# One batch of eight in two halves of d_ff, around its neighbour, with the order of the attention steps written out

## The chip, the cores and the metric

One NeuronCore of one Trainium2 chip runs the whole program. Times are device microseconds; a time of a kernel is the median of several executions, and a profile is one execution more. The engines named are PE (TensorE; PEld is its weight load), DVE (VectorE), ACT (ScalarE), POOL (GpSimd) and SP (the sync engine, whose queue, SPq, issues nearly all DMAs).

## The reference

Attention in two steps with 32 packed queries, then a gated feed-forward layer on all 4608 tokens, everything in float32:

```python
def sm_attn(qq, kk, vv):
    s = scale * np.matmul(qq, kk.transpose(0, 1, 3, 2))
    s = s - np.max(s, axis=-1, keepdims=True)
    a = np.exp(s)
    a = a / (np.sum(a, axis=-1, keepdims=True) + 1e-09)
    return np.matmul(a, vv)
p_packed = sm_attn(p, k, v)                  # 8 batches, 8 heads, 576 tokens, 64 wide
out = sm_attn(q, p_packed, p_packed)
...
g = x @ w_gate                               # x: the attention's rows, 4608 x 512
silu = g * (1.0 / (1.0 + np.exp(-g)))
val = x @ w_val
return (silu * val @ w_out).astype(np.float32)   # d_ff is 1536
```

## The kernel before

**Batches and chunks.** The batches are worked off one after another. d_ff is cut into 12 chunks of 128 columns (`fc`). In each chunk a batch's tokens come as two pieces, A (256 columns) and B (320). `gv_chunk` (L414) makes 12 matmuls for each piece, six for the gate into one PSUM bank and six for the value into a second; the two banks (`ps_gv`, two buffers) are all that there are. The gate bank is freed by ACT's Silu (`sg`, L435), the value bank by DVE's product (`hf`, or `h` where it is kept, L438). The result is split into a high part (`hh`, ACT, L79) and a low part (`hl`, DVE, L85), and `out_mm` (L446) adds it into four accumulators (`acc`) with three matmuls for each 128 tokens.

**The matrix M.** `m_part` (L390) multiplies the packed values with the weights (`w`, L164) and splits the product into `mh` (ACT) and `ml` (DVE). The second attention's weights are `a2h` and `a2l`, so gate and value are products of M and these.

**Weights.** They arrive as 64-bit words and are made into float32 on the core. `f64_convert` (L95) is two passes on ACT (L101, L102) and three on DVE (L103, L104, L105), each over 1024 columns. There are 12 conversions of gate and value weights (`w0` and so on) and 6 of output weights (`wo_f`), which are then split as well, the low part on POOL. Staging tiles (`st`), k and q share four buffers, so a load on SP's queue waits until one is free.

**Batch 0** runs through all 12 chunks of gate and value first and keeps every product (L545 to L567). Each chunk converts a further weight. A second loop (L570 to L583) then makes all output matmuls. **Batches 1 to 7** (L586 on) do the output matmuls of chunk fc-1 between the pieces of chunk fc. `aux_of(b)` (L466) is the next batch's attention as a generator; a step is taken at each `next(aux)`, twice a chunk. Its last step, at L492 to L497, is the second softmax on both halves at once, over 1152 columns. Every other batch ends with 36 matmuls for rows that both of a pair share (L621 to L628, the rest).

**Order.** PE's order is the written one (`manual_schedule`). On the other engines a scheduler places instructions, and `keep_in_program_order` pins one.

Of the kernel before, what the change touches and what calls it, by code (L numbers as in the profile page):

```python
# [26 lines left out]
SC, NSC = 96, 6  # L27
# [14 lines left out]
def tile_pack_attention_swiglu(ctx: ExitStack, tc: tile.TileContext, qT, kT, v, vq, pT, wgv, wout, out):  # L42
# [19 lines left out]

    wide = [True]
    turn = [0]

    def sooner():
        return tc.high_priority(offset=100)

    def ps():
        turn[0] += 1  # L70
        if wide[0] and turn[0] % 2:
            return ps_acc.tile([P, 512], F32, tag="acc", name="acc_aux")
        if wide[0] and turn[0] % 4:
            return ps_gv.tile([P, 512], F32, tag="gv", name="gv_aux")
        return ps_aux.tile([P, 512], F32, tag="aux", name="aux")

    def copy(e, dst, src):
        if e is nc.scalar:
            e.copy(dst, src)  # L79
        else:  # L80
            e.tensor_copy(dst, src)

    def split(dst_h, dst_l, src, hi=nc.scalar, lo=nc.vector):
        copy(hi, dst_h, src)
        lo.tensor_tensor(dst_l, src, dst_h.bitcast(F32), op=ALU.subtract)  # L85
# [4 lines left out]
    def f64_load(src):  # L90
        st = io_tile([P, 1024, 2], I32, "st")
        nc.sync.dma_start(st.rearrange("p n two -> p (n two)"), src)
        return st

    def f64_convert(dst, st, shape):  # L95

        lo, hi = (st[:, :, i].rearrange("p (a n) -> p a n", a=shape) for i in range(2))
        d = dst.bitcast(I32)  # L100
        nc.scalar.activation(dst, hi.bitcast(F32), AF.Abs)  # L101
        nc.scalar.activation(lo.bitcast(F32), lo.bitcast(U32), AF.Identity, bias=minus_two, scale=LOW_WORD)  # L102
        nc.vector.tensor_scalar(dst, dst, F64_HI_LEAST, F64_HI_MOST, op0=ALU.max, op1=ALU.min)  # L103
        nc.vector.scalar_tensor_tensor(d, d, 3, lo, op0=ALU.logical_shift_left, op1=ALU.bitwise_or)  # L104
        nc.vector.scalar_tensor_tensor(d, hi, 0x3FFFFFFF, d, op0=ALU.bitwise_or, op1=ALU.bitwise_and)  # L105
# [6 lines left out]
    def convert_w(fc):  # L112
        f64_convert(w_t[fc // 2][:, :, fc % 2, :], sts.pop(fc), NHP)

    def load_wout(fc):
        sto[fc] = io_tile([P, 1024, 2], I32, "st")
        nc.sync.dma_start(
# [3 lines left out]
    def convert_wout(fc):  # L121
        f = wos[fc] = pool.tile([P, 2, DM], F32, tag="wf", bufs=1, name="wo_f")
        f64_convert(f, sto.pop(fc), 2)

    def slot(dtype, name):
        return pool.tile([P, DM], dtype, tag="slot", bufs=2 * NFC + 2, name=name)
# [11 lines left out]
    def load_k(b):  # L138
        p_t = pool.tile([P, NHP, NP], F32, tag="p", bufs=2, name="p_t")
        (nc.sync if b else nc.scalar).dma_start(p_t, pT[b])  # L140
        k_t = io_tile([P, 2, NHP, HS], F32, "k_t")
        for hf in range(2):
            nc.sync.dma_start(k_t[:, hf], kT[b, :, hf])
        kps[b] = (k_t, p_t)

    def load_v(b):
        if b < NEARLY:
            vs[b] = pool.tile([SC, NSC, H * D], F32, tag="v", bufs=1, name="v_t")
            nc.sync.dma_start(vs[b], v[b])
        else:  # L150
            vs[b] = pool.tile([P, NPAR, NHP, NKQ, D], F32, tag="v", bufs=1, name="v_t")
            nc.sync.dma_start(vs[b], vq[b - NEARLY])

    def load_q(b):
        qs[b] = io_tile([P, 2, NHP, HS], F32, "q_t")
        for c in range(2):
            nc.sync.dma_start(qs[b][:, c], qT[b, :, c])
# [8 lines left out]
    def s1_scores(b, direct):  # L166
# [21 lines left out]
        if direct:  # L188
# [6 lines left out]
            nc.vector.tensor_tensor(rs[:, 0], rs[:, 1], rs[:, 2], op=ALU.add)  # L195
# [8 lines left out]
    def s1_post(b):  # L204
        t1, rs, _ = st1.pop(b)
        nc.vector.tensor_scalar(rs[:, 1], rs[:, 0], 1e-9, None, op0=ALU.add)
        nc.vector.reciprocal(rs[:, 2], rs[:, 1])
        a1 = pool.tile([SC, NPAR * NSC, P], F32, tag="a1", bufs=1, name="a1")
        for i in range(0, NPAR * NSC, 4):
            p_t = ps()  # L210
            for x in range(4):
                par, c = divmod(i + x, NSC)
                nc.tensor.transpose(p_t[:SC, x * P : (x + 1) * P], t1[:, par, c * SC : (c + 1) * SC], ident)
            copy(
                nc.vector if wide[0] and i == 4 else nc.scalar,
                a1[:, i : i + 4], p_t[:SC].rearrange("p (c x) -> p c x", x=P),
# [4 lines left out]
        for par in range(NPAR):  # L221
            for c in range(NSC):
                for hp in range(NHP):
# [3 lines left out]
                        a1[:, par * NSC + c, 32 * hp : 32 * hp + 32],  # L227
                        v_t[:, c, h * D : (h + 1) * D],
                        start=(c == 0),
                        stop=(c == NSC - 1),  # L230
                    )
        pp = pool.tile([P, NPAR, D], F32, tag="pp", bufs=1, name="pp")
# [9 lines left out]
        ppts[b] = pool.tile([P, P], F32, tag="ppt", bufs=2, name="ppt")  # L242
        nc.scalar.copy(ppts[b], p_t[:, :P])
        yield

    sq = {}

    def q_scores(b):
# [7 lines left out]
        for g in range(2):  # L256
# [12 lines left out]
            for par in range(NPAR):  # L269
                x, m = pss[par][:, : 2 * SQ].rearrange("p (h n) -> p h n", h=2), z[:, 0, par, hs]  # L270
                nc.vector.tensor_reduce(m, x, axis=AX.X, op=ALU.max)
                nc.vector.tensor_tensor(
                    e[:, par, hs, :SQ], x, m.unsqueeze(2).broadcast_to([P, 2, SQ]), op=ALU.subtract
                )
            yield

    def q_weights(b):
# [3 lines left out]
        ev = e.rearrange("p r h n -> p (r h) n")  # L281
        nc.scalar.activation(ev[:, :, :SQ], ev[:, :, :SQ], AF.Exp, scale=SCALE)
        zv = z.rearrange("p s r h -> p s (r h)")
        nc.vector.tensor_reduce(zv[:, 1], ev[:, :, :SQ], axis=AX.X, op=ALU.add)
        x = pool.tile([P, NJ, 2, H], F32, tag="x1", bufs=1, name="x1")
        zd = dram.tile([P, 2, H], F32, tag="zd", bufs=2, name="zd")
        nc.sync.dma_start(zd, zv)
        for i in range(NJ):
            nc.sync.dma_start(x[NP * i : NP * i + NP], zd.rearrange("(j n) s h -> n j s h", j=NJ))
        for _ in range(3):  # L290
# [15 lines left out]
        nc.vector.tensor_tensor(f, t, y[:, 0, NJ], op=ALU.mult)
        nc.vector.tensor_tensor(
            ev[:, :, :SQ], ev[:, :, :SQ], f.unsqueeze(2).broadcast_to([P, H, SQ]), op=ALU.mult
        )
        a1 = pool.tile([P, NPAR, NHP, NKQ, NP], F32, tag="a1", bufs=1, name="a1")  # L310
        for par in range(NPAR):
            nc.vector.transpose(
                a1[:, par].rearrange("p h k n -> p (h k n)"), e[:, par].rearrange("p h n -> p (h n)")
            )
        sq[b] = a1
        for _ in range(2):
            yield
# [20 lines left out]
    def s2_scores(b):  # L338
        s2, _ = st2[b]
        q_t, ppt = qs.pop(b), ppts[b]  # L340
        for c in range(2):
# [5 lines left out]
            for par in range(NPAR):  # L347
                nc.vector.transpose(s2[:, c, par], pss[par][:, :HS])
# [12 lines left out]
    def s2_max(b, cs):  # L361
        x, (m, _, _), shape = s2_view(b, cs)
        nc.vector.tensor_reduce(m, x, axis=AX.X, op=ALU.max)  # L363
        nc.vector.tensor_tensor(x, x, m.unsqueeze(2).broadcast_to(shape), op=ALU.subtract)  # L364

    def s2_exp(b, cs):
        x = st2[b][0][:, cs].rearrange("p c r n -> p (c r n)")
        nc.scalar.activation(x, x, AF.Exp, scale=SCALE)
# [4 lines left out]
    def s2_norm(b, cs):  # L373
        x, (m, s, r), shape = s2_view(b, cs)
        nc.vector.tensor_reduce(s, x, axis=AX.X, op=ALU.add)  # L375
        nc.vector.tensor_scalar(m, s, 1e-9, None, op0=ALU.add)
        nc.vector.reciprocal(r, m)
        nc.vector.tensor_tensor(x, x, r.unsqueeze(2).broadcast_to(shape), op=ALU.mult)  # L378

    def s2_back(b, c):  # L380
# [3 lines left out]
        nc.vector.transpose(t.rearrange("p r n -> p (r n)"), s2[:, c].rearrange("p r n -> p (r n)"))  # L384
        at = (slice(None), slice(None), slice(c * HS, (c + 1) * HS))
        split(ah[at], al[at], t)

    ms = {}

    def m_part(b, k, fcs):  # L390
# [11 lines left out]
        for par in range(NPAR):  # L402
            at = (slice(None), par, fcs)
            split(mh[at], ml[at], pss[par][:, :n].rearrange("p (f n) -> p f n", n=2 * P))
# [3 lines left out]
    def h_split(src, hi, lo):  # L408
        hh = pool.tile([P, 256], F32R, tag="hh", bufs=3, name="hh")
        hl = pool.tile([P, 256], F32R, tag="hl", bufs=3, name="hl")  # L410
        split(hh, hl, src, hi, lo)
        return hh, hl

    def gv_chunk(b, fc, is_b, fill, kept=None):  # L414
# [20 lines left out]
        nc.scalar.activation(sg[:, :n], pgs[0][:, :n], AF.Silu)  # L435
        hf = pool.tile([P, 256], F32, tag="hf", bufs=2, name="hf") if kept is None else kept
# [7 lines left out]
    def out_mm(acc, hh, hl, c, fc):  # L444
        for i, (h_, w_) in enumerate(((hl, wo_h), (hh, wo_l), (hh, wo_h))):
# [4 lines left out]
                start=(fc == 0 and i == 0),  # L450
                stop=(fc == NFC - 1 and i == 2),
            )

    def emit_out(acc, row, eng):
        ot = pool.tile([P, DM], F32, tag="ot", bufs=2, name="ot")
        copy(nc.scalar if eng else nc.vector, ot, acc)
        nc.sync.dma_start(out[row : row + P, :], ot)
# [3 lines left out]
    def run_all(*gens):  # L461
        for g in gens:
            for _ in g:
                pass

    def aux_of(b):  # L466

        d = b + 1
        if d == B:
            return  # L470
        if d < NEARLY:
            yield from s1_scores(d, False)
            if d + 1 < B:
                load_k(d + 1)
# [3 lines left out]
        else:  # L478
            yield from q_scores(d)
            yield from q_weights(d)  # L480
            if d + 1 < B:
# [4 lines left out]
        if d + 1 < B:  # L486
            load_v(d + 1)
        s2_tiles(d)
        yield from s2_scores(d)
        if d + 1 < B:  # L490
            load_q(d + 1)
        s2_max(d, both)  # L492
        s2_exp(d, both)
        s2_norm(d, both)
        s2_a2(d)
        for c in range(2):
            s2_back(d, c)  # L497

    with tc.manual_schedule(engines={mybir.EngineType.PE}):

        load_k(0)
        load_w(0)
        load_v(0)
        load_q(0)
        load_w(1)
        s1 = s1_post(0)
        run_all(s1_scores(0, True))
        for _ in range(3):
            next(s1)
        convert_w(0)  # L510
        run_all(s1)
        load_w(2)
        s2_tiles(0)
        s2_a2(0)
        run_all(s2_scores(0))
        for c in range(2):
# [149 lines left out]
```

## Time and profile before

| | us |
|---|---|
| median of 3 runs (797.18 to 799.49) | 799.23 |
| the profiled execution, its own time | 797.01 |
| its span | 795.2 |
| from the start to batch 0's first gate matmul | 30.09 |
| batch 0, chunks, then outputs | 30.09 to 109.78, to 150.90 |
| batch 1 | 150.90 to 239.63 |
| the rest of batches 0 and 1 | 239.63 to 247.79 |
| batch 2 | 247.79 to 335.91 |
| batch 7, no attention beside it | 705.23 to 783.20 |

The span is what the profile covers; the execution's own time is 1.8 us longer. A stretch is read by its length against PE's busy time in it. PE's order is fixed, so an idle PE names the work that was late.

### The profile page before, as it was taken

The numbers are of one execution on the slowest core, as the hardware profiler recorded it, in microseconds if no ns is written. First come the engines' busy times: TensorE is split into PE (matmuls) and PEld (weight loads), VectorE is DVE, ScalarE is ACT, GpSimd is POOL, SyncE is SP. The second block draws the span as 40 slices with busy tenths as digits, with TensorE's granted clock in tenths as the row PEclk, the third lists the DMA queues.
The fourth block names the chain that finished last, engine by engine and source line by source line (L and its number), as shares of the span: only waits on it lengthen the run. The fifth ranks groups of instructions, "written<-read, shape, count | busy, mean of one in ns | idle before, by whom it ended". The sixth has DMA issues, their size and how long they took to land.

```text
span 795.2 us, 14294 instructions
## 1 busy us (share of the span) xinstructions
PE 743.4 (93%) x5866; PEld 599.5 (75%) x5866; DVE 454.1 (57%) x968; ACT 349.8 (44%) x665; POOL 19.5 (2%) x25
## 2 busy tenths in 40 slices
PE   5579789999999999999999999999999999999998
PEld 3357567787788877878788777878778877888886
DVE  3998777455745656355745557455554556443434
ACT  3688664453532625354432445335442444343331
POOL 0001122000000000000000000000000000000000
PEclk9999998999999999999999999999999999999999
DMA  9957742221101230021101211010101000010001
GB/s 316 305 202 266 259 161 74 100 66 67 61 1 67 66 106 22 27 92 68 60 1 67 67 67 61 1 55 3 68 1 53 16 2 1 2 54 2 1 1 66
DMA packets 19776, 59.09 MB, mean 74 GB/s; under 512 B 5952, under 2 KB 6976, under 8 KB 17216
## 3 DMA queue, kind: packets, MB, share of 16 engines
q1 hardware_dynamic: 19568, 58.12, 20.9%
q8 instruction: 46, 0.75, 0.4%
q14 instruction: 18, 0.15, 0.1%
q10 hardware_dynamic: 144, 0.07, 0.0%
HBM read 48.69 MB, written 9.49 MB: 73 GB/s over the span
## 4 chain that ended last, share of the span: by engine, by line
PE 72%; DVE 15%; ACT 8%; DMA 2%; issue 2%; POOL 0%; SPq 0%; DVEq 0%; ACTq 0%
PE gv L428 31%; PE acc L446 27%; PE aux L164 6%; PE aux L446 4%; DVE ml L85 2%; PE aux L325 2%; DMA v_t<-in_v 2%; DVE r L375 1%; DVE s L378 1%; DVE r L363 1%; ACT L435 1%; DVE s L364 1%; DVE w L104 1%; PE aux L262 1%; DVE hf L438 1%
## 5 line engine op out<-in xcount | busy, mean ns | idle before, releaser
L428 PE MATMUL gv<-a2h,ml 128*128 128x256 f32 (+1 forms) x768 | 175.8, 311 | 28.4 <-DVE t L441 9.2
L428 PEld LDWEIGHTS gv<-a2h,ml 128*128 128x128 f32 x768 | 128.8, 191 | 65.6 <-issue 23.0
L428 PE MATMUL gv<-a2l,mh 128*128 128x256 f32 (+1 forms) x768 | 166.7, 299 | 0.9 <-DVE a2l L85 0.9
L428 PE MATMUL gv<-a2h,mh 128*128 128x256 f32 (+1 forms) x768 | 166.1, 298 | 0.0
L435 ACT ACTIVATE sg<-gv 128x256 f32<-128x256 f32 x192 | 78.8, 411 | 191.2 <-PE gv L428 140.0
L446 PE MATMUL acc<-wo_h,hl 128*128 128x512 f32 x384 | 157.0, 409 | 4.1 <-DVE hl L85 4.1
L438 DVE TENSOR_TENSOR hf<-gv,sg 128x256 f32<-128x256 f32 x168 | 71.1, 423 | 155.8 <-PE gv L428 153.1
L446 PE MATMUL acc<-wo_l,hh 128*128 128x512 f32 x384 | 151.8, 395 | 0.0
L446 PE MATMUL acc<-wo_h,hh 128*128 128x512 f32 x384 | 151.1, 394 | 0.0
L79 ACT CAST hh<-hf 128x256 fp32r<-128x256 f32 x168 | 68.1, 405 | 143.4 <-DVE hf L438 143.4
L428 PEld LDWEIGHTS gv<-a2l,mh 128*128 128x128 f32 x768 | 125.4, 192 | 1.5 <-DVE a2l L85 1.5
L428 PEld LDWEIGHTS gv<-a2h,mh 128*128 128x128 f32 x768 | 125.6, 192 | 0.0
L446 PEld LDWEIGHTS acc<-wo_h,hl 128*128 128x128 f32 x384 | 72.8, 189 | 51.1 <-issue 35.7
L85 DVE TENSOR_TENSOR hl<-hf,hh 128x256 fp32r<-128x256 f32 x168 | 70.4, 419 | 52.8 <-ACT hh L79 52.8
L446 PEld LDWEIGHTS acc<-wo_h,hh 128*128 128x128 f32 x384 | 72.7, 189 | 16.7
L446 PEld LDWEIGHTS acc<-wo_l,hh 128*128 128x128 f32 x384 | 72.9, 190 | 9.5
L85 DVE TENSOR_TENSOR ml<-aux,mh 128x512 fp32r<-128x512 f32 (+1 forms) x106 | 63.0, 630 | 13.1 <-ACT mh L79 12.9
L164 PE MATMUL aux<-w,ppt 64*32 64x512 f32 (+1 forms) x848 | 56.1, 564 | 4.2 <-ACT t L184 4.0
L79 ACT CAST mh<-aux 128x512 fp32r<-128x512 f32 (+1 forms) x106 | 52.2, 546 | 8.0 <-PE aux L164 2.9
L435 ACT ACT_TABLE_LOAD x21 | 26.9, 1283 | 0.7
L102 ACT ACTIVATE st<-st,minus_two 128x1024 f32<-128x1024 uint32 x18 | 22.4, 1246 | 0.6 <-DMA st<-in_wout 0.6
L164 PEld LDWEIGHTS aux<-w,ppt 64*32 64x32 f32 x848 | 10.4, 106 | 13.5 <-ACT t L184 5.0
(127 smaller groups left out, 591.2 us busy)
## 6 DMA issues: line engine op xcount, KB each, us to landing
st<-in_wgv SPq DMA_DIRECT2D x12, 1024.0 KB, 6.0
k_t<-in_kT SPq DMA_DIRECT2D x16, 576.0 KB, 4.9
q_t<-in_qT SPq DMA_DIRECT2D x16, 576.0 KB, 4.7
out<-ot SPq DMA_DIRECT2D x36, 256.0 KB, 2.1
v_t<-in_vq SPq DMA_DIRECT2D x6, 1280.0 KB, 5.7
st<-in_wout SPq DMA_DIRECT2D x6, 1024.0 KB, 6.1
v_t<-in_v SPq DMA_DIRECT2D x2, 1152.0 KB, 12.6
p_t<-in_pT SPq DMA_DIRECT2D x7, 64.0 KB, 3.0
```

The source lines that it names most:

```text
L79: e.copy(dst, src)
L85: lo.tensor_tensor(dst_l, src, dst_h.bitcast(F32), op=ALU.subtract)
L102: nc.scalar.activation(lo.bitcast(F32), lo.bitcast(U32), AF.Identity, bias=minus_two, scale=LOW_WORD)
L104: nc.vector.scalar_tensor_tensor(d, d, 3, lo, op0=ALU.logical_shift_left, op1=ALU.bitwise_or)
L164: nc.tensor.matmul(outs[par][32 * hp : 32 * hp + 32], lhs(r, hp), rhs(r, hp), start=True, stop=True)
L262: nc.tensor.matmul(pss[par][NP * j : NP * j + NP, i * SQ : (i + 1) * SQ], p_t[r, 2 * g + i, :], k_t[r, j // 2, 2 * g + i, j % 2 * SQ : j % ...
L325: nc.tensor.matmul(p_p[D * par : D * par + D, NP * hp : NP * hp + NP], v_t[:, par, hp, k, :], a1[:, par, hp, k, :], start=(k == 0), stop=( ...
L363: nc.vector.tensor_reduce(m, x, axis=AX.X, op=ALU.max)
L428: nc.tensor.matmul(pg[:, :n], m_[:, g, f, s * P : (s + 1) * P], a_[:, g, off : off + n], start=(i == 0), stop=(i == 5),)
L435: nc.scalar.activation(sg[:, :n], pgs[0][:, :n], AF.Silu)
L438: nc.vector.tensor_tensor(hf, pgs[1][:, o : o + 256], sg[:, o : o + 256], op=ALU.mult)
L446: nc.tensor.matmul(acc[:, :], h_[:, c : c + P], w_[fc], start=(fc == 0 and i == 0), stop=(fc == NFC - 1 and i == 2),)
```

## The change

1. **Batch 0 in two halves.** Chunks 0 to 5 of batch 0 run first, with the output matmuls two chunks behind and attention 1 in between; the four accumulators are copied out and written to DRAM (`part`). Batch 1 follows with all 12 chunks. Then batch 0's chunks 6 to 11; `part` is read back and added when its rows are written.
2. **Conversions.** Six of the twelve gate and value weights and half of the output weights are converted ahead of or in the first half; the others one step at a time in batch 1 (`convert_some`), two or three steps at a tick.
3. **Prologue.** DVE's and ACT's order is written out. v comes ahead of the first weight, on 128 partitions in place of 96. 29 matmuls on the identity (`warm_up`) stand where PE waits.
4. **Later attentions.** Their DVE, ACT and DMA instructions are pinned. Both softmaxes are cut in halves, one step a tick, and each exponential follows a Silu (`late`). That makes five exponentials a batch in place of three.

```diff
+    def pin(ins):
+        return tc.keep_in_program_order(ins) if steady[0] else ins
...
+            late.append(lambda hs=hs: pin(nc.scalar.activation(e[:, :, hs, :SQ], e[:, :, hs, :SQ], AF.Exp, scale=SCALE)))
...
         nc.scalar.activation(sg[:, :n], pgs[0][:, :n], AF.Silu)
+        if late:
+            late.pop(0)()
...
-        s2_max(d, both)
-        s2_exp(d, both)
-        s2_norm(d, both)
...
+        for c in halves:
+            s2_max(d, c)
+            late.append(lambda c=c: s2_exp(d, c))
+            yield
+        low = lambda: None
+        for c in halves:
+            low()
+            s2_sums(d, c)
+            yield
+            s2_scale(d, c)
+            low = s2_back(d, c.start)
+            yield
...
+        lo, hi = range(NFC // 2), range(NFC // 2, NFC)
...
             gv_chunk(0, fc, False, fill, kept[fc][:, :256])
+            if fc > 1:
+                outs_kept(fc - 2, 0, h, fill)
+                h = split_kept(fc - 2, 1)
             gv_chunk(0, fc, True, fill, kept[fc][:, 256:])
...
+        part = dram.tile([P, 4, DM], F32, tag="part", bufs=1, name="part")
+        for i in range(4):
+            emit_out(accs[i], part[:, i], i % 2)
...
+        def tick_one(fc, n):
+            convert_some(3 if n == 8 else 2)
...
+            if fc > 6:
+                next(aux)
...
+        whole(1, range(NFC), accs, tick_one, lambda: m_part(0, len(lo) // 2, both))
...
+        back = io_tile([P, 4, DM], F32, "part")
+        load(back, part)
...
+        whole(0, hi, accs, lambda fc, n: next(aux, None), lambda: m_part(2, 0, both))
```

In the rows below a name's number is its buffer; line numbers of the changed kernel are its own. DVE ahead of batch 0's second chunk, before:

```order
L85 TENSOR_TENSOR a2l_224<-t2_283,a2h_223 128x2x288
L85 TENSOR_TENSOR ml_253<-aux_339,mh_252 128x256
L85 TENSOR_TENSOR ml_253<-aux_340,mh_252 128x256
L438 TENSOR_TENSOR h0_306<-gv_332,sg_353 128x256
L103 TENSOR_SCALAR w1_82<-w1_82 128x4x256
L104 SCALAR_TENSOR_TENSOR w1_82<-w1_82,st_287 128x4x256
```

And now:

```order
L423 TENSOR_TENSOR a2l_96<-t2_322,a2h_95 128x2x288
L118 SCALAR_TENSOR_TENSOR w0_81<-st_111,w0_81 128x4x256
L115 TENSOR_SCALAR w1_82<-w1_82 128x4x256
L116 SCALAR_TENSOR_TENSOR w1_82<-w1_82,st_155 128x4x256
L118 SCALAR_TENSOR_TENSOR w1_82<-st_155,w1_82 128x4x256
L115 TENSOR_SCALAR w1_82<-w1_82 128x4x256
L430 TENSOR_TENSOR ml_254<-aux_378,mh_253 128x256
L116 SCALAR_TENSOR_TENSOR w1_82<-w1_82,st_290 128x4x256
L430 TENSOR_TENSOR ml_254<-aux_379,mh_253 128x256
```

The low parts of M for the second chunk came right behind `a2l`; now six passes of three conversions stand in between or ahead of the second of them. PE at the end of batch 0's chunks, before:

```order
L428 MATMUL gv<-a2h,ml 128x320 x2
L428 MATMUL gv<-a2l,mh 128x320 x2
L428 MATMUL gv<-a2h,mh 128x320 x2
L428 MATMUL gv<-a2h,ml 128x320 x2
L428 MATMUL gv<-a2l,mh 128x320 x2
L428 MATMUL gv<-a2h,mh 128x320 x2
L164 MATMUL aux<-q_t,ppt 32x288 x8
L446 MATMUL acc<-wo_h,hl 128x512
L446 MATMUL acc<-wo_l,hh 128x512
```

And in the third chunk of the first half now:

```order
L183 MATMUL aux<-w_82,ppt 32x256 x8
L474 MATMUL gv<-a2h,ml 128x256 x2
L474 MATMUL gv<-a2l,mh 128x256 x2
L474 MATMUL gv<-a2h,mh 128x256 x2
L494 MATMUL acc<-wo_h,hl 128x512
L494 MATMUL acc<-wo_l,hh 128x512
L494 MATMUL acc<-wo_h,hh 128x512
L494 MATMUL acc<-wo_h,hl 128x512
L494 MATMUL acc<-wo_l,hh 128x512
L494 MATMUL acc<-wo_h,hh 128x512
L183 MATMUL aux<-k_t,p_t 32x288 x8
```

Output matmuls, all behind the last chunk before, now stand between the pieces. ACT in batch 2, at the second softmax of attention 3, before:

```order
L435 ACTIVATE sg_3162<-gv_3132 128x256
L368 ACT_TABLE_LOAD
L368 ACTIVATE s2_3029<-s2_3029 128x1152
L79 CAST mh_3146<-aux_3148 128x512
L79 CAST mh_3146<-aux_3149 128x512
L79 CAST hh_3166<-hf_3164 128x256
L435 ACT_TABLE_LOAD
L435 ACTIVATE sg_3190<-gv_3176 128x320
```

And now:

```order
L481 ACTIVATE sg_3252<-gv_3238 128x320
L401 ACT_TABLE_LOAD
L401 ACTIVATE s2_3148<-s2_3148 128x576
L91 CAST hh_3258<-hf_3255 128x256
L481 ACT_TABLE_LOAD
L481 ACTIVATE sg_3300<-gv_3270 128x256
L401 ACT_TABLE_LOAD
L401 ACTIVATE s2_3148<-s2_3148 128x576
L447 CAST mh_3284<-aux_3286 128x512
L447 CAST mh_3284<-aux_3287 128x512
L91 CAST hh_3305<-hf_3303 128x256
L481 ACT_TABLE_LOAD
```

One exponential of 1152 columns became two of 576 behind two Silus that follow each other, each with a table load on either side.

## Rows read from the trace of the kernel before

**Rows 1.** Busy time by stretches, whole core: start and end, length, then for each engine busy us (and instructions), the granted clock, the DMA share and GB/s. The stretches are the prologue, batch 0's first chunk, its other eleven, its outputs, batch 1, the rest, batch 2, batch 7.

```profile
0.00:30.09 30.09, 11.49 (x189) 6.63 (x189) 16.98 (x34) 15.64 (x27) 0.74 (x7) 1.00 0.96 332
30.09:38.07 7.98, 7.04 (x41) 5.41 (x41) 7.95 (x14) 3.60 (x7) 0.00 (x0) 1.00 0.75 220
38.07:109.78 71.71, 58.60 (x600) 44.55 (x598) 59.01 (x107) 53.60 (x92) 9.04 (x7) 0.95 0.65 230
109.78:150.90 41.12, 37.04 (x168) 28.49 (x161) 28.55 (x43) 19.43 (x36) 8.67 (x6) 0.92 0.28 102
150.90:239.63 88.73, 86.76 (x706) 70.28 (x705) 49.93 (x112) 38.98 (x75) 0.20 (x1) 1.00 0.16 57
239.63:247.79 8.16, 8.16 (x39) 6.76 (x38) 3.48 (x9) 0.59 (x1) 0.00 (x0) 1.00 0.30 110
247.79:335.91 88.12, 86.31 (x707) 70.12 (x706) 48.68 (x108) 37.88 (x73) 0.20 (x1) 1.00 0.15 49
705.23:783.20 77.97, 77.88 (x513) 66.68 (x513) 31.08 (x76) 25.93 (x60) 0.00 (x0) 1.00 0.04 15
```

**Rows 2.** Who waited for whom, PE alone, whole span: the waiting instruction, what ended the wait, us in total, times, longest us.

```profile
PE gv L428 <- DVE t L441: 9.2, 6, 1.5
...
PE gv L428 <- ACT sg L435: 4.7, 6, 1.8
PE gv L428 <- DVE h L438: 4.2, 5, 1.4
PE acc L446 <- DVE hl L85: 4.1, 1, 4.1
```

**Rows 3.** DVE's groups by line and shape, whole span: busy us, mean ns of one, and idle time before.

```profile
L104 DVE SCALAR_TENSOR_TENSOR w<-w,st 128x1024 int32<-128x1024 int32 x12 | 14.7, 1221 | 0.9 <-ACT st L102 0.7
L105 DVE SCALAR_TENSOR_TENSOR w<-st,w 128x1024 int32<-128x1024 int32 x12 | 14.6, 1214 | 0.1
...
L438 DVE TENSOR_TENSOR h<-gv,sg 128x256 f32<-128x256 f32 x24 | 10.0, 417 | 5.1 <-PE gv L428 4.2 <-ACT sg L435 1.0
...
L384 DVE STREAM_TRANSPOSE t<-s 128x576 f32<-128x576 f32 x16 | 12.3, 768 | 0.0
...
L103 DVE TENSOR_SCALAR w<-w 128x1024 f32<-128x1024 f32 x12 | 9.1, 768 | 4.1 <-ACT w L101 4.1
L85 DVE TENSOR_TENSOR ml<-aux,mh 128x256 fp32r<-128x256 f32 x22 | 8.5, 419 | 0.4 <-ACT mh L79 0.2
...
L375 DVE TENSOR_REDUCE r<-s 128x18 f32<-128x576 f32 x2 | 1.5, 746 | 0.0
```

**Rows 4.** DVE in order of time in the prologue: start, us, instruction.

```profile
22.45 0.42 DVE L85 TENSOR_TENSOR ml<-gv_aux,mh 128x256 fp32r<-128x256 f32 x1
22.79 0.41 DVE L85 TENSOR_TENSOR ml<-acc_aux,mh 128x256 fp32r<-128x256 f32 x1
...
34.19 1.18 DVE L105 SCALAR_TENSOR_TENSOR w<-st,w 128x1024 int32<-128x1024 int32 x1
...
37.67 1.23 DVE L104 SCALAR_TENSOR_TENSOR w<-w,st 128x1024 int32<-128x1024 int32 x1
```

**Rows 5.** PE in order of time in batch 0: the second chunk's first piece, and a wait with what follows it (in brackets the idle time before and what ended it).

```profile
38.07 0.40 PE L428 MATMUL gv<-a2h,ml 128*128 128x256 f32 x2
...
59.78 0.95 PE L164 MATMUL aux<-w,ppt 64*32 64x256 f32 x16 [2.10 <-ACT t L184]
...
61.95 0.73 PE L428 MATMUL gv<-a2h,ml 128*128 128x320 f32 x2
```

**Rows 6.** ACT's waits, whole span: the copy of an accumulator waiting for its output buffer.

```profile
ACT ot L79 <- DMA out<-ot: 11.5, 8, 2.3
```

**Rows 7.** PE in order of time: a whole part of M, the scores and the packing of a later attention.

```profile
710.17 1.09 PE L164 MATMUL aux<-w,ppt 64*32 64x512 f32 x16
159.01 1.25 PE L262 MATMUL aux<-k_t,p_t 64*32 64x144 f32 x32
280.42 2.52 PE L325 MATMUL aux<-a,v_t 128*64 128x32 f32 x80
```

**Rows 8.** DVE and PE in order of time in batch 2, at the second softmax.

```profile
304.77 1.34 DVE L378 TENSOR_TENSOR s<-s,r 128x1152 f32<-128x1152 f32 x1
306.03 0.42 DVE L438 TENSOR_TENSOR hf<-gv,sg 128x256 f32<-128x256 f32 x1
307.39 0.47 PE L428 MATMUL gv<-a2h,ml 128*128 128x256 f32 x2 [1.54 <-DVE t L441]
```

**Rows 9.** ACT in order of time in batch 2, at the first softmax's exponential.

```profile
261.54 0.38 ACT L435 ACTIVATE sg<-gv 128x256 f32<-128x256 f32 x1 [2.06 <-DVE z L271]
261.94 1.28 ACT L282 ACT_TABLE_LOAD   x1
263.23 1.17 ACT L282 ACTIVATE e<-e 128x1152 f32<-128x1152 f32 x1
264.30 0.39 ACT L79 CAST hh<-hf 128x256 fp32r<-128x256 f32 x1
264.71 1.28 ACT L435 ACT_TABLE_LOAD   x1
266.00 0.44 ACT L435 ACTIVATE sg<-gv 128x320 f32<-128x320 f32 x1
```

**Rows 10.** SP's queue in order of time in batch 2: maxima and sums go to DRAM (zd) and come back (x).

```profile
265.81 0.33 SPq L287 DMA_DIRECT2D zd<-z  x1
267.75 1.75 SPq L289 DMA_DIRECT2D x<-zd  x4
```

More of the change, by code (lines that the diff above doesn't have):

```diff
@@ L26 @@
 NFC = DF // P
-SC, NSC = 96, 6
+NSC = -(-S // P)
 NJ, SQ = 4, S // 4
@@ new lines, in begin, with rest @@
+    def begin(b):
+        odd = b % 2
+        if b // 2 not in t4:
+            t4[b // 2] = pool.tile([P, NFC, P], F32, tag="t4", bufs=1, name="t4")
+        row0 = (b // 2) * 2 * S
+        rows = [row0 + P * t for t in ((7, 8, 5, 6) if odd else (0, 1, 2, 3))]
+        return rows, [ps_acc.tile([P, 512], F32, tag="acc", name="acc") for _ in range(4)]
+    def rest(b):
+        p4 = ps()
+        t4_t = t4.pop(b // 2)
+        for fc in range(0, NFC, 2):
+            h = h_split(t4_t[:, fc : fc + 2].rearrange("p f t -> p (f t)"), nc.vector, nc.vector)
+            for i in range(2):
+                out_mm(p4, *h, i * P, fc + i)
+        row = (b // 2) * 2 * S + 4 * P
+        emit_out(p4, out[row : row + P], 0)
@@ new lines, in tile_pack_attention_swiglu, with convert_some @@
+        work = None
+        asked = 1
+        def convert_some(n):
+            nonlocal work, asked
+            for _ in range(n):
+                while work is None or next(work, 0) == 0:
+                    if not todo:
+                        return
+                    while asked < min(len(todo), 3):
+                        todo[asked][0](todo[asked][2])
+                        asked += 1
+                    work = todo.pop(0)
+                    asked -= 1
+                    work = work[1](work[2])
@@ new lines, in tile_pack_attention_swiglu, with then @@
+        _, accs = begin(0)
+        back = io_tile([P, 4, DM], F32, "part")
+        load(back, part)
+        load_k(3)
+        whole(0, hi, accs, lambda fc, n: next(aux, None), lambda: m_part(2, 0, both))
+        run_all(aux)
+        load_q(3)
+        for i, r in enumerate(rows):
+            emit_out(accs[i], out[r : r + P], 0, back[:, i])
+        rest(1)
+        for b in range(2, B):
+            rows, accs = begin(b)
+            if b + 1 < B:
+                aux = attention(b + 1)
+            def then():
+                if b + 1 < B:
+                    m_part(b + 1, 0, both)
+            whole(b, range(NFC), accs, lambda fc, n: next(aux, None), then)
```

485 lines of the change are left out of this document (275 added, 210 removed).

## The prediction

> **What bounds the kernel now.** I read the windows by stage first, PE's waits second, then the order of time inside the stages where PE waits, and last the groups of DVE and ACT, which give prices. In the windows [rows 1], compare PE's busy time with the length of each stretch. Batch 7, with nothing beside it, takes 77.97 us, 77.88 of them busy at a granted clock of 1.00: PE is the bound there and nothing on another engine can help. Batch 2 is 8.43 us busier (attention 3 and a part of M) and loses 1.8 us. The loss sits at the start: 30.09 us until the first gate matmul, then 79.7 us for chunks that hold about half of batch 0's matmuls. In 38.07 to 109.78 PE is idle for 71.71 - 58.60 = 13.1 us, and the clock of .95 says that some of its busy time was at the lower level too. DVE is busy 59.01 us there, ACT 53.60: neither is full, yet PE waits on both. In batch 0's outputs PE is idle 4.1 us more, in one wait for the low part of a kept product [rows 2]. So batch 0 costs 30.09 to 150.90 = 120.8 us, where a bare batch costs 78.
>
> PE's other waits are small: 9.2 us in six for `t`, the second half of the softmax's product [rows 2]. Batch 2 shows what lies behind one: a pass of 1.34 us over 1152 columns stands ahead of the product that frees the value bank, and PE idles 1.54 us [rows 8].
>
> **The change part by part.**
>
> *Start to batch 0's second chunk.* It begins at 38.07 [rows 5]. v arrives earlier, so the first exponential does, and the first chunk's first piece may begin some 4 us sooner. But PE's second chunk needs the low part of M, and ahead of that DVE still has its list: by 38 us it had finished three conversions and begun a fourth [rows 4]; now three whole ones and two passes of a fourth stand ahead. The list is the same, so I take 38 as unchanged; bounds 35 to 41 (the gain of the early piece at most; or one conversion, 0.77 + 1.22 + 1.21 = 3.20 us [rows 3], more). The 29 warm-up matmuls stand where PE is free (11.49 us busy of 30.09 [rows 1]) and cost nothing; without that cover they would cost some 3 us, at half of the .20 that one of 256 columns takes [rows 5].
>
> *First half, from 38 us to batch 1.* DVE's list here: five conversions of 3.20 and one last pass, 17.2 us; 31 products and low parts of .42, 13.0; six products of the shared rows at half that, 1.3; two softmax halves, each four passes like the 746 ns reduce, two like the 768 ns transpose and .4 of small ones, 9.8; eight maxima and transposes of 288 columns, estimated at .46 each, 3.7; small ones .9. Together 45.9 us over 82 instructions, at the durations of [rows 3]. Neighbours overlap: two low parts of .42 start .34 apart [rows 4]; .08 on each of 82 leaves 39.3. In the stretch before, with the same mix of work, DVE was busy 59.01 of 71.71 us [rows 1], a share of .823. At that share the list takes 39.3/.823 = 47.8 us with the overlap taken off, 45.9/.823 = 55.8 without, so batch 1 would begin at 86 or 94. PE has about half a batch, 39 us, and some attention, so it isn't the bound. ACT's list is about as long as DVE's. At the end four accumulators are copied out through two buffers; ACT has waited up to 2.3 us for such a buffer [rows 6]. Batch 1 uses the same banks, so I add one for that to the middle, 90: batch 1's first gate matmul at **91**, range 84 to 97 (109.78 + 41.12 after it was the old end of the whole batch).
>
> *Batch 1.* A bare batch, 77.97 [rows 1]; a whole part of M for batch 0's second half, 1.09; two groups of scores of attention 2, 2 x 1.25 [rows 7]: 81.6 us of PE. Six conversions and half of the output weights are beside it. DVE has 49.93 us in batch 1 before [rows 1]; six conversions add 19 and part of an attention leaves, so 65 to 74 of some 85, where the first loop ran at .82. In that loop a value bank was needed back after 12 matmuls of the next piece; here output matmuls lie between, so each eviction has about 78/24 = 3.2 us. Idle time for this: from 0 to the 13.1 us that the first loop lost over eleven converting chunks. I take 4, since the spacing is roughly double. Batch 1: 85.6, to 176.6.
>
> *Batch 0's second half.* Half of 77.97, 39.0; a part of M for batch 2, 1.09; packing 2.52; the product with q at 1.25 [rows 7]; and what is left of an attention's 8.43 us, 1.07. Sum 44.9, to 221.5. The read of `part` (1 MB) is asked for well ahead and DMA is busy for a sixth of such a stage [rows 1]: nothing. The adds replace copies on DVE. Then the rest, 8.16 as before: 229.7 in place of 247.79, so **-18.1**.
>
> *Batches 2 to 6.* The 1.34 us pass becomes two, and `t` no longer stands behind it: the 1.8 us that a batch loses falls to about .6, five times -1.2 = **-6**; bounds -8.5 (all of it) and +4 (the new stalls below). The exchange through DRAM keeps its length: zd is issued at 265.81 and the last of x at about 269.5 [rows 10], and the reduction that waits for x is now pinned about one chunk, 6.5 us, behind; if x is late, the products queued behind it on DVE wait about a microsecond, which the second value bank covers. ACT gets two more exponentials a batch, with two more loads before and two after them: 4 x 1.28 = 5.1 us [rows 9] on an engine busy 37.88 of 88.12 [rows 1].
>
> The row bears on that last price: the Silu after the exponential's load pair starts 4.46 us after the one before, and PE doesn't wait for it; the exponential starts as its load ends, 261.94 + 1.28 = 263.22 [rows 9].
>
> The Trainium skill, page "ScalarE: Activation LUTs", section "What ACT_TABLE_LOAD costs", gives each switch about 2.66 us, a load of 1283 ns and then a drain of 1380, and its section on table sets wants calls of one set batched, which speaks against cutting exponentials in halves between Silus. The load agrees with the row; the drain isn't seen there. By the page ACT would get 10.6 us a batch rather than 5.1, and the Silus around a pair would be late.
>
> *The last batch* has no attention beside it: nothing changes.
>
> Sum: -18.1 - 6 = -24.1. The profiled execution took 797.01 us, so 772.9, rounded to **773**; it lies 2.2 us below the median of the runs, 799.23, which I leave in the range.
>
> **The rivals.**
>
> *All engines keep pace.* DVE's list then runs without gaps (43 us from 38: batch 1 at 81), batch 1 has no stalls and batches 2 to 6 lose nothing: 773 - 10 - 4 - 2.5 = 756. For it: conversions no longer stand in PE's way in the written order. Against: in the old loop DVE never passed .82.
>
> *The split exponentials surface on PE.* Two half exponentials follow each other, one for each Silu. A piece then costs ACT .38 + 1.28 + .59 + .39 + 1.28 = 3.9 us [rows 9], two 7.8, against a chunk of 6.5 on PE; with two casts of M, .8, ACT is 2.1 behind. Before, the spare bank hid such a delay. If it doesn't, two pairs a batch lose 4.2 in place of 1.8: 5 x 2.4 = +12 in place of -6, so 791. By the section on table sets in the Trainium skill, page "ScalarE: Activation LUTs", this is what would happen, with drains on top.
>
> *It doesn't do what it says.* The conversions in the first half, with a whole attention and maxima between them, keep PE waiting as in the old loop, and batch 1 starts at 109 as the outputs did: +18, 791.
>
> *Slower: the conversions pinned into batch 1 hold its evictions.* In the old loop a 2.10 us wait is followed by matmuls of 320 columns at .73 where the .40 of 256 columns gives .50 [rows 5]: the lower clock. If each of nine converting chunks has one such wait and some 3.4 us at half rate after it (1.7 lost), batch 1 loses 9 x 3.8 = 34 in place of 4: +30, 803. It decides from (4 + 26)/9 = 3.3 us lost in each converting chunk. Against it: .42 us products wait for at most one conversion pass, 1.22 us, since two or three passes stand at a tick with products between.
>
> **How the numbers follow.** Forecast 773, with its own range of 764 to 782: .53. All keep pace, 756: .17. Split exponentials, 791: .12. Not what it says, 791: .10. Slower, 803: .06. Within 0.3% (2.4 us, about what a measurement of this kernel can tell from no change): .02. The range takes in the forecast's own and, two us beyond 756 and 791, most of the fast case and of the two middle rivals: 754 to 793. Faster by over 0.3%: .53 + .17 + .12 + .10 = .92; slower .06.
>
> **What would show it.** Right: second chunk near 38, batch 1's first gate matmul near 91, end of the rest near 230, batches 2 to 6 some 87 us each, and PE's wait for `t` gone from its list. If batch 1 starts past 100, the first half is as bound by the conversions as the old loop was; a clock under .95 there says that PE's gaps cost twice. Many waits of PE on `h` or `sg` in batch 1 mean that conversions stand ahead of evictions. ACT's Silu named as releaser in batches 2 to 6, at pairs of table loads, means that the split cost more than the pass of 1152. It would be wrong altogether if PE were busy for less of the first half than of the old loop, 58.60 of 71.71 us.

## The result and the profile after

The changed kernel takes 803.76 us (median of 4 runs, 803.33 to 804.35) against 798.25 for the kernel before beside it (797.18 to 799.49): ratio 1.008, 95% interval 1.0062 to 1.0098. It is slower by 0.8%, and the interval lies clear of 1. The forecast of 773 and its range, up to 793, missed. The profiled execution took 803.33 us, its span 801.5.

Windows by stage of the changed kernel, columns as in [rows 1]: prologue and first pieces, the second chunk on, batch 1, batch 0's second half, the rest, batch 2, batch 7.

```profile
26.01:37.88 11.87, 6.95 (x44) 4.84 (x42) 11.45 (x18) 8.30 (x11) 0.00 (x0) 0.71 0.47 170
37.88:104.74 66.86, 52.74 (x427) 38.15 (x427) 48.51 (x88) 41.96 (x72) 9.87 (x7) 0.87 0.30 105
104.74:200.60 95.86, 87.33 (x593) 70.97 (x593) 64.03 (x123) 57.05 (x95) 7.63 (x6) 0.93 0.38 133
200.60:247.25 46.65, 44.42 (x377) 35.80 (x376) 27.58 (x64) 21.21 (x40) 0.20 (x1) 1.00 0.35 134
247.25:255.53 8.28, 8.28 (x36) 6.83 (x37) 4.19 (x12) 0.00 (x0) 0.00 (x0) 1.00 0.23 87
255.53:343.46 87.93, 86.76 (x705) 70.42 (x704) 49.49 (x116) 43.09 (x79) 0.20 (x1) 1.00 0.14 48
711.24:789.38 78.14, 78.05 (x513) 66.83 (x512) 31.12 (x76) 25.92 (x60) 0.00 (x0) 1.00 0.04 14
```

Set against the forecast's own stages:

| stage | forecast, us | measured, us | off |
|---|---|---|---|
| second chunk begins | 38 | 37.88 | 0 |
| batch 1's first gate matmul | 91 | 104.74 | +13.7 |
| batch 1 | 85.6 | 95.86 | +10.3 |
| batch 0's second half and the rest | 44.9 + 8.16 | 46.65 + 8.28 | +1.9 |
| start of batch 2 to start of batch 7 | 457.4 - 6 | 455.71 | +4.3 |

The last batch adds 0.2 (78.14 for 77.97). Together 30.4, and 772.9 + 30.4 = 803.3. Batch 2 begins at 255.53 in place of 247.79, 7.7 us late; batches 2 to 6 give back 1.7.

PE's waits in the changed kernel, whole span, as in [rows 2]:

```profile
PE gv L474 <- ACT sg L481: 10.0, 14, 3.8
PE acc L494 <- DVE hl L95: 4.6, 4, 2.8
PE gv L474 <- DVE h L486: 4.0, 2, 2.9
...
PE aux L183 <- ACT t L203: 3.1, 1, 3.1
PE aux L183 <- DVE w L118: 1.8, 1, 1.8
```

The wait for `t` of [rows 2], 9.2 us, is gone as forecast (the `t` of L203 is another tile). In its place Silu (`sg`) is late 14 times for 10.0 us, where it had been 4.7 in six: three times in batch 1, once in batch 0's second half, and twice in each of batches 2 to 6. One of these is 3.8 us long, in batch 1. ACT there, in order of time, and then windows before, in and after the stretch that follows:

```profile
166.34 0.41 ACT L91 CAST hh<-hf 128x256 fp32r<-128x256 f32 x1 [1.60 <-DVE hf L486]
166.65 1.13 ACT L111 ACTIVATE w<-st 128x1024 f32<-128x1024 f32 x1
167.68 1.21 ACT L113 ACTIVATE st<-st,minus_two 128x1024 f32<-128x1024 uint32 x1
168.90 1.28 ACT L306 ACT_TABLE_LOAD   x1
170.20 0.68 ACT L306 ACTIVATE e<-e 128x576 f32<-128x576 f32 x1
170.90 1.28 ACT L481 ACT_TABLE_LOAD   x1
172.19 0.44 ACT L481 ACTIVATE sg<-gv 128x320 f32<-128x320 f32 x1
```

```profile
164.00:171.00 7.00, 4.50 (x23) 3.41 (x21) 3.70 (x8) 5.34 (x8) 0.00 (x0) 0.99 0.39 152
171.00:181.00 10.00, 6.56 (x32) 4.32 (x33) 6.90 (x12) 6.08 (x9) 0.00 (x0) 0.50 0.01 1
181.00:200.00 19.00, 19.00 (x119) 16.22 (x119) 12.94 (x32) 9.37 (x18) 2.54 (x2) 1.00 0.02 3
```

From 166.34 to the Silu at 172.19 ACT has 5.9 us of work in a row: a cast, two passes of a conversion, and an exponential with a table load on either side, none of them waiting for another engine once the cast has begun. PE runs dry, and then works ten microseconds at a granted clock of .50, the 1.2 GHz level.

The first half, cut in three:

```profile
38.00:61.00 23.00, 16.17 (x112) 11.06 (x113) 20.89 (x30) 15.50 (x23) 5.19 (x3) 0.71 0.67 232
61.00:86.00 25.00, 23.08 (x253) 17.40 (x253) 15.18 (x34) 16.50 (x34) 4.47 (x4) 1.00 0.12 44
86.00:105.00 19.00, 13.63 (x67) 9.76 (x66) 12.58 (x26) 10.09 (x17) 0.20 (x1) 0.91 0.08 28
```

DVE is full first (20.89 of 23 us), then PE (23.08 of 25), then nobody: the second softmax of attention 1 goes from engine to engine. Here a transpose on DVE is cast on ACT, the low part of it waits for that cast, and behind it stands the low part that PE waits for:

```profile
92.20 0.77 DVE L420 STREAM_TRANSPOSE t<-s 128x576 f32<-128x576 f32 x1
93.01 0.67 ACT L422 CAST a2h<-t 128x576 fp32r<-128x576 f32 x1 [1.66 <-DVE t L420]
93.71 0.76 DVE L423 TENSOR_TENSOR a2l<-t,a2h 128x576 fp32r<-128x576 f32 x1 [0.74 <-ACT a2h L422]
94.39 0.75 DVE L95 TENSOR_TENSOR hl<-h,hh 128x256 fp32r<-128x256 f32 x2
94.86 0.50 PE L494 MATMUL acc<-wo_h,hl 128*128 128x512 f32 x1 [2.77 <-DVE hl L95]
```

No average over the half shows that.

### The profile page after: what moved, and what is told of

Its sections match the earlier page's. It is cut to its first block, busy times and chain, and to the rows that moved or that the text cites. A ratio compares the mean times of both kernels' runs of the same rounds, so it can differ in the third digit from the quotient of the medians.

```text
span 801.5 us, 14316 instructions
## 1 busy us (share of the span) xinstructions
PE 754.6 (94%) x5840; PEld 608.7 (76%) x5840; DVE 463.2 (58%) x1022; ACT 382.8 (48%) x696; POOL 19.3 (2%) x25
## 4 chain that ended last, share of the span: by engine, by line
PE 69%; ACT 13%; DVE 7%; issue 3%; DMA 0%; DVEq 0%; ACTq 0%
PE gv L474 31%; PE acc L494 25%; PE aux L183 6%; PE aux L494 4%; ACT L481 4%; PE aux L358 2%; ACT hh L91 2%; ACT sg L481 1%; DVE ml L430 1%; ACT mh L447 1%; ACT L401 1%; ACT L306 1%; ACT st L113 1%; DVE hf L486 1%; PE aux L293 1%
## 5 line engine op out<-in xcount | busy, mean ns | idle before, releaser
L486 DVE TENSOR_TENSOR hf<-gv,sg 128x256 f32<-128x256 f32 x180 | 75.8, 421 | 149.2 <-PE gv L474 124.5
L91 ACT CAST hh<-hf 128x256 fp32r<-128x256 f32 x180 | 72.7, 404 | 129.8 <-DVE hf L486 129.8
L95 DVE TENSOR_TENSOR hl<-hf,hh 128x256 fp32r<-128x256 f32 x180 | 76.2, 423 | 89.1 <-ACT hh L91 88.7
L183 PE MATMUL aux<-w,ppt 64*32 64x512 f32 (+1 forms) x800 | 54.9, 603 | 4.9 <-ACT t L203 3.1
L481 ACT ACT_TABLE_LOAD x34 | 43.6, 1283 | 11.0 <-issue 10.3
L91 ACT COPY ot<-acc 128x512 f32<-128x512 f32 x16 | 9.4, 589 | 24.9 <-PE acc L494 15.5
```

The lines of the kernel that those rows point to most:

```text
L91: return e.copy(dst, src) if e is nc.scalar else e.tensor_copy(dst, src)
L95: pinned(lo.tensor_tensor(dst_l, src, dst_h.bitcast(F32), op=ALU.subtract))
L183: nc.tensor.matmul(outs[par][32 * hp : 32 * hp + 32], lhs(r, hp), rhs(r, hp), start=True, stop=True)
L486: nc.vector.tensor_tensor(hf, pgs[1][:, o : o + 256], sg[:, o : o + 256], op=ALU.mult)
```

## The experiments

Times are medians; each ratio is against the kernel before, run beside it, with its 95% interval. Where a batch begins or ends is its first gate matmul in PE's order of time.

**Batch 1 without its conversions.**

```
-        load_w(6)
...
+        todo = []
+        for j in range(NFC // 4, NFC // 2):
+            w_t[j] = w_t[j - NFC // 4]
+        for fc in hi:
+            wo_h[fc], wo_l[fc] = wo_h[fc - len(lo)], wo_l[fc - len(lo)]
```

> The changed kernel without the nine conversions in batch 1 and their loads: chunks 6 to 11 use the weights of chunks 0 to 5 again. Theory A: batch 1's 95.9 us are PE's own 81.6 and what the conversions cost, waits and the half clock that follows; without them batch 1 takes 82 to 84 and the whole about 791. Rival B: attention 2's pinned exponentials hold the Silus by themselves, as in the steady batches: batch 1 stays above 88 and the whole above 796.

Measured 790.11 us, ratio 0.9907 (0.9886 to 0.9928). Its batch 1:

```profile
103.92:186.82 82.90, 81.88 (x592) 67.87 (x593) 39.30 (x96) 35.59 (x71) 0.00 (x0) 1.00 0.15 53
```

Theory A: 82.9 us, the clock at 1.00 throughout, the exponentials still there. So the conversions, with their loads, cost batch 1 95.86 - 82.90 = 13.0 us; no wait of PE in batch 1 names a load. PE's idle time there falls from 8.5 to 1.0 us, by 7.5. The other 5.5 is busy time, 87.33 against 81.88, and most of that is the lower clock: half of the 3.4 us after 106 and of the 6.66 us that PE works between 170.9 and 181.1, an estimated 5.0. The first of these two stretches follows a wait that this run has too, without a fall of the clock (see the last section), so it can't be put down to the conversions: they cost 11 to 13 us.

**Attention 2 two chunks later.**

```
-            if fc > 6:
+            if fc > 8:
                 next(aux)
...
+            for _ in range(2 if turn[0] in (2, 4, 5, 9) else 1):
+                next(aux, None)
```

> The changed kernel with attention 2 begun in batch 1's chunk 9 in place of 7, four steps of it doubled up in batch 0's second half. Theory A: in the trace after, PE waits 3.8 us for sg at 172 us because two conversion passes, an exponential and two table loads stand ahead of that Silu on ACT, and the clock at half for 10.2 us from 170.9 comes from that wait; with the exponentials two chunks later both go, batch 1 takes 87 to 89 us in place of 95.9, the whole 796. Rival B: the conversions alone hold the evictions; batch 1 stays above 93 and the whole above 801.

Measured 806.69 us, ratio 1.0109 (1.0093 to 1.0126). Batch 1 took 90.2, nearer to theory A (87 to 89) than to rival B (above 93): the 3.8 us wait is gone and half clock lasts 3.4 us there in place of 10.2. But the steps doubled up behind it took more than that back: PE waits 2.9 us for `a`, the attention's weights, and the second half with the rest takes 65.5 us where it took 54.9, at a granted clock of .92. Neither of the two places was free.

**Three steps at every tick.**

```
-            convert_some(3 if n == 8 else 2)
+            convert_some(3)
```

> The changed kernel with three steps of a conversion at both ticks of a chunk in batch 1, in place of two and three. Theory A: the last gate and value weight is then converted by chunk 7, so the wait of M for it (1.8 us at 177) goes and little is left to meet the exponentials of chunk 7: batch 1 near 90, the whole near 798. Rival B: denser conversions hold more products and Silus: batch 1 stays at 95 or grows.

Measured 800.38 us, ratio 1.0033 (1.0023 to 1.0043); batch 1 92.9. Between the two theories: the wait of M for its weight goes, and so does the long stretch at half clock; 3.3 us of waits for `t` (L489) behind denser conversions come.

**M early at the seam, which is where batch 0's first half ends and batch 1 begins; and one weight more converted there.** The first edit alone, then with the rest and three steps a tick:

```
+        m_part(1, 0, both)
         for fc in lo[-2:]:
...
-        m_part(1, 0, both)
```

```
+            if fc == 5:
+                load_w(6)
+                load_w(7)
...
+        run_all(convert_w(6))
```

> The changed kernel with batch 1's first part of M ahead of the last 24 output matmuls of the first half in place of behind them. Theory A: the end of the half waits in a chain, outputs, M, its low part, first gate matmul; with M early PE's 1.8 us idle at 103 to 105 goes and batch 1 starts at 103 in place of 104.7, the whole 802. Rival B: what M's casts take from ACT and DVE ahead of the second softmax delays that by as much: no change within 1 us.

> The changed kernel with M early as in the run before, three steps at both ticks, and one weight more converted at the end of the first half, where DVE was idle from 97 to 105, its load asked for in chunk 5. Theory A: three causes of batch 1's 14 us are then out of the way together: batch 1 starts at 103 to 104 and takes 86 to 88, the whole 793 to 795, below the kernel before. Rival B: the conversion at the seam holds batch 1's first products and the dense ones the later: 800 or more.

M early: 800.43 us, ratio 1.0035 (1.002 to 1.0049). Batch 1 begins at 103.2, and the half clock that had followed the wait at 104.74 is gone too, so it gains 3.3, more than expected. With the rest: 796.19 us, ratio 0.9981 (0.9968 to 0.9993), a little below the kernel before. Its batch 1 takes 89.67 us at full clock, where 86 to 88 was expected:

```profile
103.40:193.07 89.67, 83.50 (x594) 67.72 (x592) 63.35 (x120) 55.11 (x93) 8.02 (x6) 1.00 0.38 136
```

DVE and ACT are busy nearly as long as in the changed kernel (63 and 55 us for 64 and 57), though one conversion, worth some 1.4 us by the run above, has moved to the seam; so where the work stands makes most of the 6.2 us. This version, and the one with an extra tick on top of it below, do all the work and beat both kernels, if by little.

**The first half: a shorter conversion, four fewer, no attention 1.**

```
+        if not short[0]:
             yield pin(nc.vector.scalar_tensor_tensor(d, d, 3, lo, op0=ALU.logical_shift_left, op1=ALU.bitwise_or))
```

```
-            elif fc == 2:
-                run_all(convert_w(4), convert_w(5))
...
+                w_t[2] = w_t[0]
```

```
-        aux = attention(1)
+        aux = iter(())
+        a2[1], ppts[1] = a2[0], ppts[0]
```

> The changed kernel without the shift and or pass (1.22 us on DVE) in the five conversions of batch 0's first half, so those weights come out wrong; nothing else is changed. Theory A: from 38 to 61 us DVE is the bound (busy 92 of 100), so four passes there bring batch 1's first gate matmul forward by 4 to 5 us, from 104.7 to 100. Rival B: attention 1's chain on ACT and PE's own work after 61 set the end of the half; batch 1 begins less than 1.5 us earlier.

> The changed kernel without four of the five conversions of the first half (two gate and value weights, two of output weights) and their loads; chunks 2 to 5 use the weights of others again. Theory A: 12.8 us of DVE and 9.6 of ACT go, and the stretch to 61 us is bound by DVE, but attention 1's chain and PE's own work remain behind it: batch 1's first gate matmul comes 6 to 9 us earlier, at 96 to 99. Rival B: conversions are all that holds the half: 90 or less. Rival C: the chain of attention 1 is: above 102.

> The changed kernel without attention 1 and its loads; batch 1 uses batch 0's packed values and second attention again. Theory A: DVE's conversions hold the half until 61 us, and from there attention 1's two softmaxes do, one step after another on ACT, DVE and PE; without them batch 1's first gate matmul comes 12 to 18 us earlier, at 87 to 93. Rival B: conversions and output matmuls take as long by themselves: not below 98.

Batch 1's first gate matmul, in the kernels with four conversions fewer and without attention 1:

```profile
96.79 0.39 PE L474 MATMUL gv<-a2h,ml 128*128 128x256 f32 x1 [1.58 <-DVE ml L430]
```

```profile
89.22 0.38 PE L474 MATMUL gv<-a2h,ml 128*128 128x256 f32 x1 [1.57 <-DVE ml L430]
```

The short conversions bring it to 101.65: 3.1 us for five passes of 1.22, between the theories (798.96 us, ratio 1.002, 1.0008 to 1.0033). Four conversions fewer bring 7.95 us for 12.8 of DVE, theory A (795.3 us, ratio 0.9977, 0.9959 to 0.9995). Leaving attention 1 out brings 15.5, theory A again (786.67 us, ratio 0.9864, 0.9843 to 0.9885). So a microsecond of conversion on DVE costs .5 to .6 there. An attention, with a part of M, makes a steady batch 88.12 - 77.97 = 10.2 us longer [rows 1]; attention 1 makes this half 15.5 longer.

**Attention 1 a chunk earlier**, on the last kernel with M early (three steps a tick, one weight converted at the seam).

```
-                if fc and count[0] in (4, 6, 8):
+                if count[0] in ((2, 4), (2, 4, 6, 8))[fc > 1] and fc:
```

> The last kernel of the runs before (M early, a conversion at the seam, three steps a tick in batch 1) with attention 1 a chunk earlier: two steps in chunk 1 and four in each later one, in place of one and three. Theory A: the second softmax then lies beside the outputs of chunks 2 and 3 on PE and the wait of 2.9 us near 95 and the half clock behind it go: batch 1 starts 3 to 5 us earlier, the whole 791 to 793. Rival B: DVE is full until 61, so an earlier step only waits in front of PE's matmuls: no gain, or up to 3 us slower.

Measured 799.53 us, ratio 1.0022 (1.0008 to 1.0036): batch 1 begins at 106.5 in place of 103.4. That is rival B's size, but not its cause: from the second chunk to batch 1 PE is idle 12.4 us, in that kernel 12.9. What grows is PE's busy time, from 52.7 to 56.4 us, at a granted clock of .93 from 61 to 86 us and .83 after, where it had been 1.00 and .90.

**No warm-ups.**

```
-            for _ in range(n):
+            for _ in range(0):
```

> The changed kernel without the 29 warm-up matmuls. Theory A: they stand where PE waits, and PE is at half clock again by 17 us, so they are worth nothing: within 1 us of 803.8. Rival B: without them the first chunk's matmuls run at half clock and batch 1 begins 2 to 4 us later. Rival C: with them the clock falls at 17 and at 31 us where before it stayed up from 37 to 61; without them the time falls by 2 us or more.

Measured 804.32 us, ratio 1.008 (1.0067 to 1.0092), batch 1 at 104.89: theory A. The first gate matmul even comes 1.9 us earlier, at 24.12, but its pair takes .80 us in place of .48 and the second chunk begins 1.5 us later; by batch 1 the two kernels are level. DVE's list in between, which both have to work off, would account for that; no run shows it by itself.

**The steady batches: whole exponentials, and a tick of nothing ahead of the second attention's scores.**

```
-            late.append(lambda hs=hs: pin(nc.scalar.activation(e[:, :, hs, :SQ], e[:, :, hs, :SQ], AF.Exp, scale=SCALE)))
+            if g:
+                late.append(lambda: pin(nc.scalar.activation(e[:, :, :, :SQ], e[:, :, :, :SQ], AF.Exp, scale=SCALE)))
...
+            elif c is halves[1]:
+                late.append(lambda: s2_exp(d, both))
```

```
+        if d > 2:
+            yield
         s2_tiles(d)
```

> The changed kernel with the exponentials of the later attentions whole again (three a batch, each behind one Silu), the rest of part 4 kept. Theory A: the two waits of PE for sg in each of batches 2 to 6 (0.6 and 0.4 us in the trace after) come from pairs of half exponentials behind neighbouring Silus, so they go: batch 2 to batch 3 from 87.9 to about 86.9, the whole from 803.8 to 798 or 799 (five batches of 1.0). Rival B: one load pair around 1152 columns delays the next Silu as much, so the waits stay and the time moves by less than 1.5 us.

> The same kernel as the one before without its change, with one tick of nothing ahead of the second attention's scores from attention 3 on. Theory A: in the trace after the first q products (1.24 us for 16, the next 16 take 0.71) wait for an aux bank that M's low part still reads; a tick later they don't: 0.5 us in each of five batches, the whole 2 to 3 us faster than the 796.2. Rival B: the second exponentials move with them onto other Silus and the sum stays within 1 us.

PE in batch 2 of the changed kernel, the first q products and two waits; and DVE ahead of the q products, where the low part of M reads an `aux` bank.

```profile
275.30 0.50 PE L474 MATMUL gv<-a2h,ml 128*128 128x256 f32 x2 [0.62 <-ACT sg L481]
...
307.71 1.29 DVE L430 TENSOR_TENSOR ml<-aux,mh 128x512 fp32r<-128x512 f32 x2 [0.30 <-ACT mh L447]
308.52 1.24 PE L183 MATMUL aux<-q_t,ppt 64*32 64x288 f32 x16
...
327.44 0.51 PE L474 MATMUL gv<-a2h,ml 128*128 128x256 f32 x2 [0.35 <-ACT sg L481]
```

Whole exponentials: 802.89 us, ratio 1.0064 (1.005 to 1.0077). Of the two waits for `sg` one is left, .7 us, and the five batches take 454.14 in place of 455.71: 1.6 us, not 5. Batch 1, where attention 2 now has a whole exponential too, takes 2.1 us more, so that the whole moves by 0.9: rival B's size, though the waits go half the way of theory A. The extra tick: 795.54 us, ratio 0.9972 (0.996 to 0.9984), against 796.19 without it. The q products take .71 and .72 (in the kernel before both groups took .72), so the bank was what held them. But the two waits for `sg` in that batch grow from 1.0 to 1.3 us, and the five batches take 454.84 us for 455.75: rival B, and the two kernels can't be told apart by their times.

## Why the prediction was wrong

**The start and the warm-ups** were right: 37.88 for 38, and the warm-ups are worth nothing.

**The first half (+13.7) is the step that failed most**: DVE's list divided by its share of the old loop, .823. Both numbers were off. The list was too short: its passes laid end to end take 52.3 us where I had 45.9, and 48.51 busy, as a window counts them, where I had 39.3 with the overlap taken off. At .823 the measured list would still have brought batch 1 to 97, which is 6 of the 13.7 us. The other 8 are the share, which became 48.51/66.86 = .73. In the old loop conversions were spread over the whole stretch, with the first steps of attention 1 beside them. Here four of the five stand in the first 23 us, and a complete attention with two softmaxes, each a chain over ACT, DVE and PE, comes after.

That PE isn't the bound was wrong as well. My own terms gave it 39.0 + 8.43 = 47.4 us there, so the 53 of the forecast left 5.6 for all its waits and for the lower clock; measured were 14.1 us idle and a clock of .87. From 61 to 86 us PE is the bound, and it can't make up what it lost while DVE was. PE was busy for .79 of the half, less than the .82 of the old loop, which I had named as the sign of being wrong altogether.

The runs price the items: 8.0 us for four conversions, 15.5 for attention 1. By my sum these were 12.8/.823 = 15.6 and, for its softmax halves, maxima, transposes and small passes, 14.4/.823 = 17.5. So neither was priced too low; with both gone the sum would leave 20 us, where PE alone needs 39. One engine's list at one share can't price a stretch whose parts have different limits one after the other. The rival that batch 1 starts at 109 said nearly this, at a chance of .10.

**Batch 1 (+10.3)**: PE's own work was sized right, 81.6 against the 82.9 of the run without conversions. The conversions cost up to 13.0 where I took 4: 7.5 us of idle time, within my 0 to 13.1, and 5.5 of longer busy time, mostly the lower clock, for which the forecast had no term. I argued that an eviction has 3.2 us and a conversion pass takes 1.22; but ACT does conversions too, and with an exponential and its loads they come to 5.9 us ahead of one Silu. The slower rival had the mechanism, evictions held and half clock after, though I weighed it by DVE's passes alone and not by ACT's. Its size was smaller: 13.0 over nine conversions is 1.4 each, and alone it would not have decided. It took this and the first half together; that the time measured is the 803 of this rival is chance. I gave the rivals chances as if they excluded each other, while both hang on where conversions stand and both came true in part; the fault of the range is there.

**Steady batches (+4.3)**: the wait for `t` went, 1.5 us a batch, as forecast. (`t` is not a half of the softmax's product, as the prediction calls it, but the product for the shared rows; the pass of 1.34 us does stand ahead of it.) What is left in a batch I had put at .6: there are two waits for `sg`, 1.0 us, and .5 us that PE's records show as slow q products. Split exponentials are only .3 us a batch of it, by the run with whole ones.

The Trainium skill, page "ScalarE: Activation LUTs", section "What ACT_TABLE_LOAD costs", gives a switch 2.66 us with its drain, so that four fewer switches a batch would free an estimated 10.6 us of ACT. The rows above show loads of 1.28 and an exponential that starts as its load ends (168.90 and 170.20), so no drain here either, and with whole exponentials ACT is busy 5.3 us less in batch 2 (37.79 for 43.09).

**Batch 0's second half and the last batch** were right within 2 us; no wait of PE names the trip of `part` through DRAM.

Open: how much of the lower clock is cause and how much consequence in the first half. No run keeps PE fed there with all the work in place.

## What to carry to other kernels

A busy share is a property of an order, not of an engine: before a list is divided by the share of another stretch, cut the new order in the places where its mix changes, and ask of each part which engine is full, what chain is left, and how much slack the forecast leaves to the engine that you call not the bound. Work that is moved under a bound engine costs that engine time where it stands ahead of an eviction on either evicting engine; add up what ACT has in a row between two Silus as well as what DVE has. Risks that can come true together are added in one rival, not shared out over two.

## What was not expected of the hardware

One wait cost more than its length: after PE had been busy 4.50 of 7.00 us the granted clock was .50 for ten. In the kernel without conversions in batch 1, where no such wait is, it stayed at 1.00 for all of it. Without attention 1, and with four conversions fewer in the first half, that wait is 3.82 and 3.78 us long, and some 6.7 us at half clock follow.

But a shorter wait can go either way. In the changed kernel the clock fell to .50 for 3.4 us after the wait of 2.77 us at 94.86, and again after the one of 1.53 at 104.74. The kernel without conversions in batch 1 has both waits, at 95.50 and 103.92, and no fall. First its two waits, then the windows behind them, then the windows behind the two waits of the changed kernel:

```profile
95.50 0.50 PE L494 MATMUL acc<-wo_h,hl 128*128 128x512 f32 x1 [2.75 <-DVE hl L95]
103.92 0.38 PE L474 MATMUL gv<-a2h,ml 128*128 128x256 f32 x1 [1.51 <-DVE ml L430]
```

```profile
95.50:103.92 8.42, 6.91 (x40) 4.53 (x40) 4.44 (x9) 3.29 (x7) 0.20 (x1) 1.00 0.18 62
103.92:109.00 5.08, 4.78 (x32) 4.40 (x33) 2.06 (x6) 1.93 (x6) 0.00 (x0) 1.00 0.86 230
```

```profile
94.86:104.74 9.88, 8.35 (x40) 5.74 (x40) 4.43 (x9) 3.41 (x7) 0.20 (x1) 0.83 0.15 53
104.74:109.46 4.72, 4.50 (x21) 4.31 (x22) 1.40 (x3) 1.15 (x4) 0.00 (x0) 0.64 0.94 279
```

What decides, no run shows. Moving M ahead of 24 matmuls, which took away 1.8 us of waiting at 103 to 105, also took away the 3.4 us at half clock behind it; it is no proof that such a wait always has that price.

And a wait for a PSUM bank inside a run of small matmuls appears as a slow run, 1.24 against .71 us, not as idle time: the low part of M that still reads the bank ends at 309.0, in the middle of the run that starts at 308.52.
